# Two buffers lent to the attention's transposed probabilities, and six units under way in place of four, from unit 16 to unit 33

## The chip, the core and the metric

The kernel runs on one core of a Trainium2 chip. Its engines each work through a list of their own, in order: TensorE (PE, matrix products), VectorE (DVE), ScalarE (ACT), GpSimd (POOL) and SyncE (SP, which here issues nearly all transfers of the DMA). An instruction that waits holds up everything behind it on its engine. The metric is the device time of one execution in microseconds (us), lower being better.

## What is computed

Attention over hash buckets, then two dense layers of 1536 tokens:

```python
mask = q_bucket[:, :, :, None] == k_bucket[:, :, None, :]   # 6 sign bits of q @ proj, k @ proj
scores = np.where(mask, scale * np.matmul(q, k.transpose(0, 1, 3, 2)), -1e9)
attn = softmax(scores)                     # B, H, S, D = 2, 8, 768, 64
x = np.matmul(attn, v)                     # -> 1536 x 512
h = x @ w_in;  x = np.where(h > 0, h, np.exp(np.minimum(h, 0)) - 1) @ w_out     # 512 -> 2048 -> 512
h = x @ w_in2; out = (s * np.maximum(h, 0)**2 + b) @ w_out2
```

## The kernel before

Most numbers are split into a high and a low half in 16-bit floating point, and a product is then three products of halves.

**Units.** The attention is cut into 96 units: one unit is one head's 128 queries against all 768 keys. Eight units (all heads) make a chunk of 128 tokens, so there are 12 chunks. Units 0 to 15 (chunks 0 and 1) transpose their probabilities on PE. From unit 16 (`U0`) on, a unit goes through these steps:

1. `u_s`, line 384: four matmuls make the scores `s` in one of two PSUM buffers (`NS = 2`).
2. `u_soft`: DVE caps them and copies them to `p` with their extreme `mx` (line 395), POOL scales `mx` (line 396), ACT takes the exponential in place (line 397). There are three `p` buffers.
3. `u_split`: ACT writes the high half `ph` (line 416), POOL the low half (line 419), and SP issues a transposing DMA into `pt` (line 421). There are three `ph` buffers and four `pt` buffers (`PT = 4`).
4. `u_av`: 18 matmuls of `pt` with the values give the unit's share of `xacc` (line 440).

After the eighth unit of a chunk, `u_norm` divides by the sums: DVE writes `xf` (line 462) and, in chunks 0 and 1, casts the high half `xh` (line 474), POOL subtracts the low half (line 475), and SP issues two transposes (line 479; line 482 in later chunks) into the layer input `xx`. `xx` has three blocks of 512 tokens, each 128 partitions by 8192 bytes; block 0 holds chunks 0 to 3, block 1 chunks 4 to 7.

**The order.** `attention()` (line 518) is a generator. In a round it splits the last unit, runs `u_av` of the oldest unit if `nxt["lag"]` units are under way, and starts the next unit if fewer than that are. The lag is 5 for the first units, 4 from unit 16 on, and 5 again when the weights of the first layer are all in (`w1_step`, line 894, which then also lends further buffers). The first layer (`moe1`, line 613) works on blocks of 256 tokens: `up(0)` makes `h` (16 groups of 12 matmuls, line 574, two groups to a PSUM bank; two banks until the weights are in), ACT and DVE turn `h` into `g` (lines 582, 584, 591), `down(0)` makes `x2p`. `moe1` hands out credit by its matmuls: one unit for each 1.2 us of it during `up(0)`, then one for each 2.5 us. `up(0)` starts in the program when unit 15 has been through `u_av` and `u_norm`.

**Weights.** In the same stretch `w_stream` (line 184) takes in 64 weight chunks of 512 KB as 64-bit numbers: SP loads `wraw` (line 175, three buffers), DVE joins the words in three instructions (lines 213, 214, 216: `wx`, `wx`, `wa`), ACT takes the high half, and DVE (line 223: `wil`, `wol`) or POOL the low half. One step of it follows each step of the attention before `up(0)`, and later two of three slots of `moe1`.

The program is put in order at build time by a scheduler with priorities (program order) and a timing model of its own, so what stands on each engine is not quite the order of the code.

Of the kernel before, what the change touches and what calls it, by code (L numbers as in the profile page):

```python
# [7 lines left out]
F32 = mybir.dt.float32  # L8
# [10 lines left out]
PT = 4  # L19
EX = dict(p=1, ph=1, pt=1, raw=2)  # L20
NP = 3
# [17 lines left out]
NPH = 3  # L39
# [24 lines left out]
W_FROM = 3  # L64
HOLD = {(0, 2, "v"): 3, (0, 3, "v"): 4, (1, 0, "k"): 8, (1, 0, "q"): 9}
HOLD_E = []
LN2 = 0.6931471805599453


def model_kernel(tc, q, k, v, proj, w_in, w_out, w_in2, w_out2, s2, b2, sel, pop, eye, out):  # L70
    nc = tc.nc
    B, H, S, D = q.shape
# [22 lines left out]
    with ExitStack() as base:  # L95
# [13 lines left out]
        unp = right(ast, "unp", NP)  # L109
        un3 = right(ast, "un3", NPH)  # L110
        ptp = right(ast, "ptp", PT)
# [7 lines left out]
        class Ring:  # L119
            def __init__(self):  # L120
                self.sets, self.n = {}, {}
# [5 lines left out]
            def take(self, kind, shape, dt, name):  # L127
                pools = self.sets[kind]
                self.n[kind] += 1
                tag = "m" if kind == "w" else kind  # L130
                return pools[self.n[kind] % len(pools)].tile(shape, dt, tag=tag, name=name)

        class late_by:
            def __init__(self, n):
# [8 lines left out]
        ring = Ring()  # L143
# [22 lines left out]
        def behind(n):  # L166

            return tc.issue_after(w_loads[n]) if n is not None else nullcontext()
# [9 lines left out]
        def w_early(ch, x):  # L178
            t = xx[1].rearrange("p a t -> p (a t)").bitcast(I32)[:, 1024 * x:1024 * x + 1024]
            with behind(HOLD_E[x]):  # L180
                nc.sync.dma_start(out=t.rearrange("p (k n) -> p k n", k=ch[1].shape[1]), in_=ch[1])
# [193 lines left out]
        sps, pf, pt, sums, xacc = ({} for _ in range(5))  # L375
# [12 lines left out]
        def u_soft(u):  # L388
            b, c, h, hp, j = unit(u)
            gr, sl = group(u)  # L390
            if sl == 0:
                sums[gr] = sml.tile([128, H], F32, tag="sum", name="sum")
            f = ring.take("p", [128, S], F32, "p")
            mx = sml.tile([128, 1], F32, tag="mx", name="mx")
            nc.vector.tensor_scalar(f, sps.pop(u), CLAMP, None, op0=ALU.min, op1=ALU.min, accum_out=mx)  # L395
            (nc.gpsimd if U0 <= u < MXP else nc.vector).tensor_scalar(mx, mx, sm / (SQ * SQ), 10.0 * LN2, op0=ALU.mult, op1=ALU.add)  # L396
            nc.scalar.activation(out=f, in_=f, func=ACTF.Exp, scale=-sm / (SQ * SQ), bias=mx,  # L397
                                 accum_out=sums[gr][:, sl:sl + 1])
            pf[u] = f

        def u_split(u, eng):
            f = pf.pop(u)
            if u < FC * H:
                p = ps_p[0].tile([128, S], F32, tag="s", name="pT")
                for cc in range(C):
                    nc.tensor.transpose(p[:, 128 * cc:128 * cc + 128], f[:, 128 * cc:128 * cc + 128], ident)  # L406
                o = ring.take("pt", [128, S], F32, "pt")
                if eng == "act":
                    nc.scalar.activation(out=o, in_=p, func=ACTF.Copy)
                else:  # L410
                    nc.vector.tensor_copy(out=o, in_=p)
                pt[u] = o
                return
            t = ring.take("ph", [128, 2, S], F16, "ph")
            if eng == "act":
                nc.scalar.activation(out=t[:, 0, :], in_=f, func=ACTF.Copy)  # L416
            else:
                nc.vector.tensor_copy(out=t[:, 0, :], in_=f)
            nc.gpsimd.tensor_tensor(out=t[:, 1, :], in0=f, in1=t[:, 0, :], op=ALU.subtract)  # L419
            o = ring.take("pt", [128, 2 * C, 128], F16, "pt")  # L420
            nc.sync.dma_start_transpose(out=o, in_=t.rearrange("p x s -> p (x s)"))
            pt[u] = o

        def u_av(u):
            b, c, h, hp, j = unit(u)
            gr, sl = group(u)
            if sl == 0:
                xacc[gr] = ps_x.tile([128, H, D], F32, tag="x", name="xacc")
            acc = xacc[gr][:, sl, :]
            o = pt.pop(u)  # L430
            if u < FC * H:
                vv = raws[b, hp, "v"].rearrange("p h (c d) -> p h c d", d=D)
                for cc in range(C):
                    nc.tensor.matmul(acc, o[:, 128 * cc:128 * cc + 128], vv[:, j, cc, :],  # L434
                                     start=(cc == 0), stop=(cc == C - 1))
                return
            vv = vHL[b, hp]
            for z, (x, y) in enumerate(((0, 0), (0, 1), (1, 0))):
                for cc in range(C):
                    nc.tensor.matmul(acc, o[:, C * x + cc, :], vv[:, j, cc, y, :],  # L440
                                     start=(z == 0 and cc == 0), stop=(z == 2 and cc == C - 1))

        xx = [xs_.tile([128, 2 * KM, 512], F16, name=f"x{i}") for i in range(B * C // 4)]
# [11 lines left out]
        def u_norm(ch):  # L455
            sm_, acc = sums.pop(ch), xacc.pop(ch)
            rs = sml.tile([128, H], F32, tag="rs", name="rs")
            nc.vector.tensor_scalar(rs, sm_, 1e-9 * SPR, (1.0 if ch < FC else SV) / SX, op0=ALU.add, op1=ALU.mult)
            rr = sml.tile([128, H, 1], F32, tag="rr", name="rr")
            nc.vector.reciprocal(out=rr, in_=rs.rearrange("p (h o) -> p h o", o=1))  # L460
            xf = ring.take("p", [128, H, D], F32, "xf")
            nc.vector.tensor_tensor(out=xf, in0=acc, in1=rr.to_broadcast([128, H, D]), op=ALU.mult)
            if ch < FC:
                xh = per.tile([128, FC, 2, H * D // FC], F16, tag="xh", name="xh")
                fl = xf.rearrange("p (c h) d -> p c (h d)", c=FC)
                hi, lo = xh[:, :, 0, :], xh[:, :, 1, :]
            else:
                xh = per.tile([128, 2, 2, H * D // 2], F16, tag="xh", name="xh")
                fl = xf.rearrange("p (y h) d -> p y (h d)", y=2)
                hi, lo = xh[:, :, 0, :], xh[:, :, 1, :]  # L470
            if FC <= ch < C:
                nc.scalar.activation(out=hi, in_=fl, func=ACTF.Copy)
            else:
                nc.vector.tensor_copy(out=hi, in_=fl)
            nc.gpsimd.tensor_tensor(out=lo, in0=fl, in1=hi, op=ALU.subtract)
            if ch < FC:
                k2 = KM // FC
                for c in range(FC):
                    nc.sync.dma_start_transpose(out=xx[0][:, 2 * k2 * ch:2 * k2 * ch + 2 * k2, 128 * c:128 * c + 128],
                                                in_=xh[:, c].rearrange("p z n -> p (z n)"))  # L480
                return
            nc.sync.dma_start_transpose(out=xx[ch // 4][:, :, ch % 4 * 128:ch % 4 * 128 + 128], in_=xh.rearrange("p y z d -> p (y z d)"))
# [29 lines left out]
        nxt = {"s": 0, "av": 0, "soft": [], "split": [], "lag": LAG0}  # L512
# [5 lines left out]
        def attention():  # L518
            for i in range(-PRE, 0):
                for fn, a in sched.get(i, []):  # L520
                    fn(*a)
                yield
            while nxt["av"] < NU:
                if nxt["split"]:
                    u_split(nxt["split"].pop(0), SPLIT(nxt["s"]))
                u = nxt["av"]
                if u < nxt["s"] and u in pt and (nxt["s"] - u >= nxt["lag"] or nxt["s"] == NU):
                    u_av(u)
                    nxt["av"] += 1
                    if u % H == H - 1:  # L530
                        u_norm(u // H)
                        if u >= FC * H - 1:
                            done_chunks[0] = u // H + 1
                u = nxt["s"]
                if u < NU and u - nxt["av"] < nxt["lag"]:
                    if u == U0:
                        ring.use(p=[unp], ph=[un3], pt=[ptp])
                        nxt["lag"] = PT
                    u_s(u)
                    nxt["s"] += 1  # L540
                    yield
                    u_soft(u)
                    nxt["split"].append(u)
                    for fn, a in sched.get(u, []):
                        fn(*a)
                yield
# [305 lines left out]
        if True:  # L852
# [12 lines left out]
            n, early = 0, []  # L865
            co1 = w_col_chunks(lambda: wo, w_out)
            for _ in att:
                n += 1
                if len(early) < len(HOLD_E) and len(w_loads) > HOLD_E[len(early)]:
                    early.append(w_early(co1[len(early)], len(early)))  # L870
# [155 lines left out]
```

## Time and profile before

| | |
|---|---|
| median of three runs | 709.73 us (708.51 to 713.6) |
| the profiled execution | 714.04 us, of which the profile's span is 711.8 |
| PE busy | 659.6 us, 93% of the span |
| DVE busy | 520.5 us, 73% |
| ACT busy | 416.3 us, 58% |
| POOL busy | 266.1 us, 37% |
| DMA queue of SP | 88.63 MB, 57.4% of 16 engines' span |

The shares are means over stages with different limits. Up to about 75 us the kernel loads and prepares; units 16 to 33 lie at about 90 to 160 us; the rest of the attention runs beside the first layer up to about 395 us; the second layer follows. A row of waits names the engine that waited, the line, and the work whose end released it. The DMA share counts the time of packets, which can overlap on one engine, so it can exceed 1.

### The profile page before, as it was taken

How to read it: one execution, taken by the hardware profiler on the slowest of the kernel's cores; microseconds unless marked ns; L12 is line 12 of the kernel's file. 1: busy time of each engine (PE TensorE's matmuls, PEld its weight loads, DVE VectorE, ACT ScalarE, POOL GpSimd, SP SyncE). 2: the span in 40 equal slices, each digit the busy share in tenths (PEclk: the TensorE clock that was granted, in tenths of full speed). 3: DMA queues.
4: the chain of work that ended last, by engine and by line, in shares of the span. 5: the costliest groups of instructions: out<-in, count | busy, mean ns of one | idle time of the engine just before them, and what ended most of it. 6: DMA issues, size and time to landing. Idle time of an engine off the chain costs nothing.

```text
span 711.8 us, 15212 instructions
## 1 busy us (share of the span) xinstructions
PE 659.6 (93%) x6192; PEld 506.6 (71%) x6192; DVE 520.5 (73%) x893; ACT 416.3 (58%) x687; POOL 266.1 (37%) x211
## 2 busy tenths in 40 slices
PE   2598978879989999999999999999999999999998
PEld 0286857668767777888888988874444446888887
DVE  5779989998878568645644699339999626999730
ACT  2849768966778788656755333234545525555520
POOL 0136767776345469945855421311211200000000
PEclk9769999999999999999999999999999999999999
DMA  9965699999999669977668555014443000000100
GB/s 211 299 162 170 160 203 203 223 228 225 196 211 216 116 116 171 150 125 122 119 115 117 135 162 165 1 31 119 135 138 112 0 1 1 16 31 31 45 30 30
DMA packets 206805, 89.72 MB, mean 126 GB/s; under 512 B 171920, under 2 KB 203408, under 8 KB 206736
## 3 DMA queue, kind: packets, MB, share of 16 engines
q1 hardware_dynamic: 206144, 88.63, 57.4%
q8 instruction: 48, 0.79, 0.5%
q14 instruction: 21, 0.17, 0.1%
q10 hardware_dynamic: 592, 0.14, 0.1%
HBM read 43.13 MB, written 3.15 MB: 65 GB/s over the span
## 4 chain that ended last, share of the span: by engine, by line
PE 66%; DMA 10%; DVE 10%; ACT 7%; issue 5%; SPq 1%; POOL 1%; DVEq 0%; ACTq 0%; POOLq 0%
PE h L574 27%; PE y L818 15%; PE x2p L574 12%; DMA pt<-ph 6%; PE s L384 4%; PE xacc L440 3%; PE xacc L434 2%; DVE p L395 2%; ACT p L397 1%; PE pT L406 1%; ACT ph L416 1%; DMA q<-src 1%; DVE g L591 1%; DMA raw<-in_k 1%; ACT q L357 1%
## 5 line engine op out<-in xcount | busy, mean ns | idle before, releaser
L419 POOL TENSOR_TENSOR ph<-p,ph 128x768 f16<-128x768 f32 x80 | 134.6, 1686 | 79.2 <-ACT ph L416 44.3
L574 PE MATMUL h<-x,wih 128*128 128x256 f16 x768 | 131.3, 275 | 3.0 <-DVE g L591 1.5
L574 PE MATMUL h<-x,wi 128*128 128x512 f16 x576 | 124.5, 379 | 0.0
L395 DVE TENSOR_SCALAR_CACHE_REDUCE p<-s 128x768 f32<-128x768 f32 x96 | 91.0, 951 | 42.2 <-PE s L384 41.3
L397 ACT ACTIVATE p<-p,mx 128x768 f32<-128x768 f32 x96 | 89.2, 929 | 50.6 <-DVE mx L396 38.8
L818 PE MATMUL y<-wqh,a 128*128 128x256 f16 x672 | 110.3, 273 | 0.0
L818 PEld LDWEIGHTS <-a 128*128 128x128 f16 x1008 | 98.6, 98 | 11.7
L574 PE MATMUL h<-x,wil 128*128 128x256 f16 x384 | 105.4, 275 | 0.0
L574 PE MATMUL x2p<-gh,woh 128*128 128x256 f16 x384 | 104.1, 273 | 0.8 <-ACT gh L594 0.8
L574 PE MATMUL x2p<-gl,woh 128*128 128x256 f16 x384 | 104.5, 273 | 0.1
L574 PEld LDWEIGHTS <-wi 128*128 128x128 f16 x576 | 56.4, 98 | 67.7
L574 PE MATMUL x2p<-gh,wol 128*128 128x256 f16 x384 | 104.5, 273 | 0.0
L818 PE MATMUL y<-wql,a 128*128 128x256 f16 x336 | 91.1, 273 | 0.0
L384 PE MATMUL s<-k,q 128*128 128x512 f16 (+1 forms) x384 | 80.7, 335 | 8.0 <-DVE p L395 7.9
L574 PEld LDWEIGHTS <-wih 128*128 128x128 f16 x768 | 74.9, 99 | 15.2 <-issue 2.0
L574 PEld LDWEIGHTS <-woh 128*128 128x128 f16 x768 | 74.9, 98 | 11.6
L597 POOL TENSOR_TENSOR gl<-g,gh 128x512 f16<-128x512 f32 x48 | 59.0, 1229 | 61.0 <-ACT gh L594 60.7
L440 PE MATMUL xacc<-vv,pt 128*128 128x64 f16 x1440 | 57.6, 194 | 16.1 <-DMA pt<-ph 16.1
L416 ACT ACTIVATE ph<-p 128x768 f16<-128x768 f32 x80 | 66.7, 836 | 7.7 <-DMA pt<-ph 5.2
L440 PEld LDWEIGHTS <-pt 128*128 128x128 f16 x1440 | 53.5, 99 | 24.3 <-DMA pt<-ph 20.3
L610 DVE SCALAR_TENSOR_TENSOR g<-h,sbs,r 128x512 f32<-128x512 f32 x48 | 35.7, 745 | 23.6 <-ACT r L607 23.6
L384 PEld LDWEIGHTS <-q 128*128 128x128 f16 x384 | 34.5, 100 | 25.6 <-issue 10.8
(118 smaller groups left out, 1040.8 us busy)
## 6 DMA issues: line engine op xcount, KB each, us to landing
wraw<-in_moe_w_in SPq DMA_DIRECT2D x32, 512.0 KB, 3.9
wraw<-in_moe_w_out SPq DMA_DIRECT2D x32, 512.0 KB, 3.9
out<-y SPq DMA_DIRECT2D x10, 256.0 KB, 2.0
raw<-in_k SPq DMA_DIRECT2D x6, 384.0 KB, 4.8
raw<-in_q SPq DMA_DIRECT2D x6, 384.0 KB, 5.7
v<-in_v SPq DMA_DIRECT2D x4, 384.0 KB, 7.8
pt<-ph SPq DMA_TRANSPOSE x80, 4.1
x<-in_k SPq DMA_DIRECT2D x2, 384.0 KB, 5.0
```

The costliest lines, as they stand in the source:

```text
L357: nc.scalar.activation(out=o[r, j].rearrange("p c t -> p (c t)"), in_=p[r], func=ACTF.Relu, scale=sc, bias=pop_sb[r, x:x + 1])
L384: nc.tensor.matmul(p[:, a0:a1], w[b, hp][:, j, c, :], kf[:, a0:a1], start=(x == 0), stop=(x == 1))
L395: nc.vector.tensor_scalar(f, sps.pop(u), CLAMP, None, op0=ALU.min, op1=ALU.min, accum_out=mx)
L397: nc.scalar.activation(out=f, in_=f, func=ACTF.Exp, scale=-sm / (SQ * SQ), bias=mx, accum_out=sums[gr][:, sl:sl + 1])
L416: nc.scalar.activation(out=t[:, 0, :], in_=f, func=ACTF.Copy)
L419: nc.gpsimd.tensor_tensor(out=t[:, 1, :], in0=f, in1=t[:, 0, :], op=ALU.subtract)
L434: nc.tensor.matmul(acc, o[:, 128 * cc:128 * cc + 128], vv[:, j, cc, :], start=(cc == 0), stop=(cc == C - 1))
L440: nc.tensor.matmul(acc, o[:, C * x + cc, :], vv[:, j, cc, y, :], start=(z == 0 and cc == 0), stop=(z == 2 and cc == C - 1))
L574: nc.tensor.matmul(p, ws[a](kk), xs[b](kk), start=(kk == 0 and z == 0), stop=(kk == n_kk - 1 and z == 2))
L597: nc.gpsimd.tensor_tensor(out=gl, in0=t["g"], in1=gh, op=ALU.subtract)
L610: nc.vector.scalar_tensor_tensor(out=g, in0=p, scalar=sb["s"], in1=t["r"], op0=ALU.mult, op1=ALU.mult)
L818: nc.tensor.matmul(p, a[:, xa, kk, :], wq[y][:, WQ[n], kk, :], start=first and k == 0, stop=k == 3 * K2 - 1, skip_group_check=True)
```

## The change

From unit 16 on the ring of `pt` buffers gets two more: slices of 3072 bytes per partition of `xx[1]`, the second block of the layer input, into which nothing else is written before chunk 4 (units 32 to 39) is done. At the same place the lag becomes 6 in place of 4. When unit 34 starts, the ring and the lag are set back to what they were. The numbers of `p` and `ph` buffers stay (`p=0, ph=0`). Units 19, 20, 25, 26, 31 and 32 get the lent buffers.

```diff
+X1 = dict(p=0, ph=0, pt=2)
+X1_END = 34
...
+        class Guest:
+            def __init__(self, t, at, n):
+                self.t, self.at, self.n = t, at, n
+            def tile(self, shape, dt, tag=None, name=None):
...
+                t = self.t[:, self.at // 2:(self.at + n * z) // 2]
...
                     if u == U0:
+                        t, at_, sets = xx[1].rearrange("p a t -> p (a t)"), 0, {}
+                        for k_, p_, n_ in (("p", unp, NP), ("ph", un3, NPH), ("pt", ptp, PT)):
+                            sets[k_] = [p_] * n_
+                            for _ in range(X1[k_]):
+                                sets[k_].append(Guest(t, at_, 4 * S))
+                                at_ += 4 * S
+                        ring.use(**sets)
+                        nxt["lag"] = PT + X1["pt"]
+                    if u == X1_END:
                         ring.use(p=[unp], ph=[un3], pt=[ptp])
                         nxt["lag"] = PT
```

No instruction is added or taken away; the lag and the rings move instructions on every engine. Lines below 67 of the kernel before stand 2 further down in the changed one, from 133 on 19, from 537 on 28.

On SP, from the last load of `w_in` and the first of `w_out` on (`x_113` is block 0 of the layer input and `x_114` block 1, so that `x_114<-ph` is a transpose into a lent buffer), the kernel before has:

```order
L175 DMA wraw<-in_moe_w_out 128x4x256
L421 DMA_TRANSPOSE pt<-ph 128x12x128 x2
L175 DMA wraw<-in_moe_w_out 128x4x256
L479 DMA_TRANSPOSE x_113<-xh 128x4x128 x2
L421 DMA_TRANSPOSE pt<-ph 128x12x128 x3
L175 DMA wraw<-in_moe_w_out 128x4x256 x2
```

The changed one has in the same place:

```order
L194 DMA wraw<-in_moe_w_out 128x4x256
L440 DMA_TRANSPOSE pt<-ph 128x12x128 x2
L194 DMA wraw<-in_moe_w_out 128x4x256 x2
L440 DMA_TRANSPOSE pt<-ph 128x12x128
L440 DMA_TRANSPOSE x_114<-ph 128x12x128
L498 DMA_TRANSPOSE x_113<-xh 128x4x128 x2
L440 DMA_TRANSPOSE x_114<-ph 128x12x128
L194 DMA wraw<-in_moe_w_out 128x4x256 x2
```

The two transposes of chunk 1 into the layer input (`x_113<-xh`) now stand behind those of units 18 and 19 and behind one more weight load.

On DVE, from the scores of unit 18 (the first `p,mx<-s` here) to those of unit 21, the kernel before has:

```order
L395 TENSOR_SCALAR p,mx<-s 128x768
L462 TENSOR_TENSOR xf<-xacc,rr 128x512
L216 SCALAR_TENSOR_TENSOR wa<-wraw,wx 128x512
L474 CAST xh<-xf 128x2x256
L395 TENSOR_SCALAR p,mx<-s 128x768
L213 TENSOR_SCALAR wx<-wraw 128x512
L223 SCALAR_TENSOR_TENSOR wil<-wa,wih 128x512
L395 TENSOR_SCALAR p,mx<-s 128x768
L214 SCALAR_TENSOR_TENSOR wx<-wraw,wx 128x512
L395 TENSOR_SCALAR p,mx<-s 128x768
```

The changed one has, from unit 19 (the first `p,mx<-s` here) to unit 21, behind unit 18 and the two instructions `wa` and `wx`:

```order
L414 TENSOR_SCALAR p,mx<-s 128x768
L233 SCALAR_TENSOR_TENSOR wx<-wraw,wx 128x512
L242 SCALAR_TENSOR_TENSOR wil<-wa,wih 128x512
L235 SCALAR_TENSOR_TENSOR wa<-wraw,wx 128x512
L414 TENSOR_SCALAR p,mx<-s 128x768
L232 TENSOR_SCALAR wx<-wraw 128x512
L481 TENSOR_TENSOR xf<-xacc,rr 128x512
L242 SCALAR_TENSOR_TENSOR wil<-wa,wih 128x512
L233 SCALAR_TENSOR_TENSOR wx<-wraw,wx 128x512
L493 CAST xh<-xf 128x2x256
L414 TENSOR_SCALAR p,mx<-s 128x768
```

The normalisation of chunk 1 (`xf`, then the cast `xh`) now stands behind the scores of units 19 and 20 and six weight instructions.

On PE the kernel before has the scores up to unit 21, then line 440 of unit 16, 12 matmuls of `h`, line 440 of unit 17, the scores of unit 22 and 36 matmuls of `h`. The changed one has the scores up to unit 23, then line 440 of units 16, 17 and 18, 12 matmuls of `h`, line 440 of unit 19, the scores of unit 24 and the same 36 matmuls of `h`.

## Rows read from the trace of the kernel before

**Rows 1.** Stretches: length, busy PE, PEld, DVE, ACT, POOL, granted clock, DMA share, GB/s.

```profile
90.00:105.00 15.00, 10.23 (x95) 7.47 (x95) 13.65 (x26) 9.91 (x18) 11.54 (x12) 0.89 1.00 194
105.00:120.00 15.00, 13.56 (x179) 11.07 (x178) 12.87 (x22) 12.81 (x24) 9.34 (x9) 1.00 1.04 216
120.00:150.00 30.00, 26.19 (x323) 21.58 (x323) 29.83 (x52) 25.46 (x46) 25.41 (x24) 1.00 1.05 214
150.00:165.00 15.00, 11.96 (x141) 9.38 (x139) 13.15 (x24) 10.94 (x21) 9.16 (x11) 0.89 1.14 240
165.00:300.00 135.00, 125.53 (x1519) 102.54 (x1518) 100.13 (x191) 107.40 (x182) 82.74 (x59) 1.00 0.95 174
300.00:450.00 150.00, 150.00 (x1707) 131.36 (x1706) 96.82 (x186) 78.15 (x134) 71.81 (x51) 1.00 0.63 128
```

**Rows 2.** Waits of PE, 105 to 165 us: us in total, times, longest.

```profile
PE xacc L440 <- DMA pt<-ph: 7.0, 6, 2.4
PE h L574 <- DVE g L591: 1.0, 1, 1.0
```

**Rows 3.** Chain of work that ended last, 90 to 165 us: start, us, what.

```profile
99.02 4.11 DMA x<-xh
103.17 2.15 PE h L574 x18
...
124.64 5.62 DMA pt<-ph
130.31 0.70 PE xacc L440 x18
...
138.47 5.38 DMA pt<-ph
143.93 0.84 ACT ph L416
```

**Rows 4.** Timeline of DVE: start, us, work, [idle before it <- releaser].

```profile
94.14 0.69 DVE L462 TENSOR_TENSOR xf<-xacc,rr 128x512 f32<-128x512 f32 x1
94.74 0.68 DVE L216 SCALAR_TENSOR_TENSOR wa<-wraw,wx 128x512 int32<-128x512 int32 x1
95.33 0.42 DVE L474 CAST xh<-xf 128x512 f16<-128x512 f32 x1
95.67 0.95 DVE L395 TENSOR_SCALAR_CACHE_REDUCE p<-s 128x768 f32<-128x768 f32 x1
...
108.14 0.69 DVE L591 SCALAR_TENSOR_TENSOR g<-h,e 128x512 f32<-128x512 f32 x1 [2.09 <-ACT e L584]
```

**Rows 5.** Timeline of PE around the start of `up(0)`.

```profile
94.28 0.81 PE L384 MATMUL s<-k,q 128*128 128x512 f16 x4 [1.28 <-DVE p L395]
97.09 1.14 PE L440 MATMUL xacc<-vv,pt 128*128 128x64 f16 x18 [2.01 <-DMA pt<-ph]
98.05 0.61 PE L574 MATMUL h<-x,wih 128*128 128x256 f16 x2
100.36 0.69 PE L440 MATMUL xacc<-vv,pt 128*128 128x64 f16 x18
103.17 0.39 PE L574 MATMUL h<-x,wih 128*128 128x256 f16 x2 [1.48 <-DMA x<-xh]
```

**Rows 6.** Timeline of POOL there.

```profile
95.84 1.16 POOL L475 TENSOR_TENSOR xh<-xf,xh 128x512 f16<-128x512 f32 x1 [1.09 <-DVE xh L474]
```

**Rows 7.** DMA issues, 105 to 165 us, then 300 to 380: count, size, landing us.

```profile
pt<-ph SPq DMA_TRANSPOSE x16, 4.9
...
pt<-ph SPq DMA_TRANSPOSE x22, 3.8
```

**Rows 8.** Waits, 90 to 165 us, of SP's queue and of ACT.

```profile
SPq L421 <- POOL mx L396: 17.8, 9, 3.0
...
ACT ph L416 <- DMA pt<-ph: 2.0, 2, 1.1
```

More of the change, by code (lines that the diff above doesn't have):

```diff
@@ L131, in take @@
                 return pools[self.n[kind] % len(pools)].tile(shape, dt, tag=tag, name=name)
+        class Guest:
+            def __init__(self, t, at, n):
+                self.t, self.at, self.n = t, at, n
+            def tile(self, shape, dt, tag=None, name=None):
+                z = 4 if dt == F32 else 2
+                n = 1
+                for d in shape[1:]:
+                    n *= d
+                assert n * z <= self.n
+                t = self.t[:, self.at // 2:(self.at + n * z) // 2]
+                t = t.bitcast(F32) if z == 4 else t
+                if len(shape) == 3:
+                    t = t.rearrange("p (a b) -> p a b", a=shape[1])
+                return t
         class late_by:
```

## The prediction

> **What bounds the kernel now.** I read the stretches first. From 300 us on PE is busy in every microsecond [rows 1], so whatever units 16 to 33 gain or lose reaches the end of the kernel at full size: the first layer stands behind them on PE, and no engine gives it back. The profiled execution took 714.04 us, with a span of 711.8; it lies 4.3 above the median of 709.73, so I work out a difference there and carry it to the median.
>
> Between 90 and 165 us PE is idle for 4.77, 1.44, 3.81 and 3.04 us, 13.1 in all [rows 1]. Second, the waits of PE: from 105 to 165 us, 7.0 us in six waits are line 440 waiting for a transpose `pt<-ph` to land, and 1.0 is `h` waiting for `g` [rows 2]. This is what more buffers and a longer lag are aimed at: a unit's `u_av` asked of PE two units later gives its transpose two more units' time to land.
>
> Two things speak against taking the 7.0 us whole. DVE is busy 12.87, 29.83 and 13.15 us in the 60 from 105 to 165 [rows 1]: 4.15 us idle, and 0.17 in the middle 30. A unit needs its 0.95 us of DVE for its scores [rows 4], the weight chunks need theirs, and no lag shortens either. And in the chain of waits the long transposes end in two ways: at 130.31 on PE, in line 440, but at 143.93 on ACT, in line 416, which writes `ph` [rows 3]. There the unit waits for one of the three `ph` buffers to be read out, and the change lends none of those. ACT's own waits of this kind come to 2.0 us [rows 8].
>
> **The change, part by part.** It adds no instruction. The two slices of `xx[1]` are free until chunk 4 is done, and the readers of a lent buffer (line 440 of units up to 32) stand on PE long before that, so I cost the lending itself at nothing; what covers it is the distance from unit 32 to unit 39, seven units. If that were gone, one transpose of the layer input would wait for one unit's 18 matmuls, 0.69 us [rows 5].
>
> *The start, unit 16 to 24.* Here the order costs something. In the kernel before, DVE does `xf` of chunk 1 at 94.14 us and the cast `xh` at 95.33, POOL follows at 95.84, SP issues the two transposes, the second at 99.02, it lands 4.11 us later, and the 36 matmuls of `h` that need it start at 103.17 after a wait of 1.48 [rows 3 to 6]. In the changed order the scores of units 19 and 20 and six weight instructions stand ahead of `xf` on DVE, and two more weight instructions in place of one between `xf` and the cast. A weight instruction starts 0.6 us after the one before (94.14, 94.74, 95.33), a unit's scores take 0.95 [rows 4]: 6 x 0.6 + 2 x 0.95 + 0.6 = 6.1 us. DVE was never short of work there (13.65 of 15 busy [rows 1]), so no idle time swallows this. On POOL the low halves of units 18 and 19 now come before that of `xh`, and on SP their transposes and a weight load come before its two; these are done while DVE is still busy with those 6.1 us, so I add nothing for them. The 36 matmuls then start at 103.17 + 6.1 = 109.3.
>
> PE is not idle for all of that. Ahead of the 36 matmuls it now also does the scores of units 23 and 24 and line 440 of units 18 and 19: 2 x 0.81 + 2 x 0.69 = 3.0 us [rows 5], which it need not do later. The start costs 6.1 - 3.0 = 3.1 us. Bounds: nothing, if DVE alone sets the pace up to 150 us and PE catches up in its gaps; and 6.1, if the work done ahead is worth nothing, because units were fitted into gaps anyway.
>
> The scores of units 22 and 23 need one of two PSUM buffers, so they wait for DVE's scores of units 20 and 21, and line 440 of unit 16, at 97.09 before, now stands behind both: PE has a longer gap ahead of it. After its gap of 2.01 us the kernel before ran its first 12 matmuls of `h` from 98.05 to 100.36, 2.31 us [rows 5], where 18 of them later took 2.15 [rows 3], so 12 would take 1.43. The 0.9 us between are the lower of its two clock levels, 1.2 in place of 2.4 GHz, as the granted clock of 0.89 over that stretch says [rows 1]. The same matmuls run in both kernels after a gap, so I add nothing, and 0.9 to the upper bound.
>
> *Units 20 to 33.* Of the 7.0 us of waits [rows 2] I take what DVE has to spare, 4.15 us, since the nearest row to a limit is DVE's 29.83 of 30; half of it is one wait, 2.09 us at 108.14 for the first group of `up(0)` [rows 4], and in the changed order scores and weight instructions stand ahead of that `g` to fill it. The lower bound is nothing: if the `ph` buffers hold the units back, their transposes are late all the same. The upper bound is 7.0. On PE the changed order in fact puts line 440 only about one unit later than before in the middle of the stretch, and around unit 33 at the old place, because the lag falls back to 4 at unit 34.
>
> *Behind unit 34.* Lag and rings are the old ones, and the units run at most one ahead of before against the first layer. PE's idle time from 165 to 300 is 9.5 us [rows 1]; I leave it as it is.
>
> **Sum.** 3.1 - 4.15 = -1.05 us: 713.0 for the profiled execution, **708.7 us** for the median.
>
> **The rivals.** *Faster.* The waits are latency and nothing else, and the start is hidden behind DVE: 0 for the start, and all 7.0 of the waits go: 702.7. For it speaks that the wait for `pt` is by far PE's largest; against it DVE's 4.15 us and the `ph` row. The Trainium skill, "Perfetto Trace Analysis", section "Optimization Strategy", says that the same gap repeating on the engine that should be saturated can mean that there isn't buffer enough for the next tile. By that rule the six waits would go and this rival would be right; the trace agrees that the gap repeats, and does not yet show which buffer is the short one. Chance 0.22.
>
> *No gain, only the start.* The transposes are slow because the DMA is full, and two more in flight only land later. The DMA share is 1.04 to 1.14 from 105 to 165 us [rows 1], and a transpose lands in 4.9 us there against 3.8 in the quiet stretch [rows 7]. Or the `ph` buffers hold the pace. Then the change doesn't do what it says: 709.73 + 3.1 = 712.8. Against it: SP waited for POOL before issuing, 17.8 us in nine waits on one row alone [rows 8], so the queue is not always backed up. The skill's same page, section "What 'DMA-bound' means", says that where specific DMA engines or the issuing queue bind, large descriptors are what matter; by it lent buffers are worth nothing here. The trace speaks only half for it, by that wait of SP. Chance 0.22.
>
> *Slower.* The start is paid in full: `up(0)` starts 6.1 us late, the two units done ahead only fill gaps that were there, and PE runs 0.9 us more at the lower clock: 709.73 + 7.0 = 716.7. The place is the wait for `x<-xh` ahead of the 36 matmuls; it decides from the point where this wait ends later than about 107 us, 4 us later than now. For it speaks the row of 4.11 us for the landing, which nothing shortens; against it DVE's full rows behind it, in which PE has 3.81 us to catch up [rows 1]. Chance 0.16.
>
> **How the numbers follow.** The forecast has 0.40: its parts are each half certain, and it lies between the others. The range reaches to the faster and the slower rival, since signs are mixed: 703.0 to 716.7; the forecast's own is 706 to 711.5. About 1%, 7.1 us, is what a measurement of this kernel can tell from no change: under 702.6 lies near half of the faster rival, 0.11; over 716.8 some more than half of the slower one and a little of the second, 0.11; the rest, 0.78, is within.
>
> **What would show it.** The start: the cast `xh` near 101.4 us, the second `x<-xh` landing near 109, and line 440 of unit 16 behind the scores of unit 23. If the cast is at 97 or before, the 3.1 us are wrong. The middle: PE's waits for `pt<-ph` from 105 to 165 us down to about 3 us, and DVE with almost no idle time; if they stay near 7 with ACT waiting more in line 416, the `ph` buffers hold; if the landing goes from 4.9 towards 6 us, the DMA does. I am wrong in kind if PE's idle time behind 165 us moves by more than 2 us, since I gave that stretch nothing.

## The result, and the profile after

The changed kernel takes 719.16 us (median of four runs, 717.42 to 722.22), the kernel before 711.55 beside it (708.51 to 713.6): a ratio of 1.011, with a 95% interval of 1.0067 to 1.0154. It is slower by 1.1%, 7.6 us, where I had forecast 708.7 and a range up to 716.7. The profiled execution took 722.22 us, its span 720.4.

The stretches of the changed kernel, as in [rows 1] (length, busy PE, PEld, DVE, ACT, POOL, granted clock, DMA share, GB/s):

```profile
90.00:105.00 15.00, 7.95 (x78) 5.42 (x77) 14.97 (x28) 8.98 (x16) 9.99 (x12) 0.67 1.00 219
105.00:120.00 15.00, 12.89 (x146) 10.03 (x145) 11.99 (x22) 11.76 (x22) 8.17 (x8) 0.88 1.03 189
120.00:150.00 30.00, 26.10 (x325) 21.38 (x323) 28.46 (x49) 26.22 (x49) 24.60 (x24) 1.00 1.13 235
150.00:165.00 15.00, 14.21 (x174) 11.85 (x172) 14.72 (x23) 10.58 (x19) 11.91 (x11) 1.00 1.14 226
165.00:235.00 70.00, 59.44 (x661) 46.84 (x659) 50.09 (x91) 53.19 (x89) 29.69 (x25) 0.95 1.00 187
235.00:300.00 65.00, 62.35 (x784) 51.67 (x783) 41.47 (x93) 50.28 (x87) 47.20 (x32) 1.00 0.84 143
300.00:450.00 150.00, 149.17 (x1711) 129.98 (x1710) 92.84 (x187) 79.06 (x134) 72.04 (x51) 1.00 0.63 130
```

And two stretches of the kernel before, cut in the same way:

```profile
165.00:235.00 70.00, 63.94 (x742) 51.92 (x741) 57.50 (x97) 52.89 (x89) 33.95 (x26) 1.00 1.05 205
235.00:300.00 65.00, 61.59 (x779) 50.62 (x778) 42.63 (x95) 54.51 (x94) 48.79 (x33) 1.00 0.84 140
```

From 90 to 165 us PE idles 7.05 + 2.11 + 3.90 + 0.79 = 13.85 us, where it was 13.1 [rows 1]. From 165 to 235 us PE idles 10.56 us in place of 6.06 and does 661 matmuls in place of 742, part of them at the lower of its two clock levels (granted clock 0.95). That row of before is a favourable one: e3_ph2, which has its order on PE, and e9_norm_early (both below) show no loss and idle 9.34 and 9.15 us there, at a granted clock of 1.00:

```profile
165.00:235.00 70.00, 60.66 (x712) 48.74 (x709) 56.62 (x94) 53.81 (x90) 30.72 (x25) 1.00 1.00 193
165.00:235.00 70.00, 60.85 (x720) 48.73 (x719) 53.24 (x91) 53.77 (x90) 30.41 (x24) 1.00 0.97 198
```

So of that stretch the clock and 1 to 2 us of idle time belong to the change. A comparison from a point of the program is surer than one by the time since the span began. DVE's order is the same in all kernels here up to the scores of unit 18; from their start to the end of the span, before first:

```profile
93.26:711.80 618.54, 592.04 (x5724) 456.48 (x5723) 447.38 (x738) 354.55 (x588) 228.61 (x172) 0.99 0.55 115
91.16:720.40 629.24, 596.70 (x5724) 458.96 (x5723) 441.65 (x738) 355.04 (x588) 227.65 (x172) 0.98 0.54 113
```

PE does the same 5724 matmuls in 10.7 us more: 6.0 us more idle time (32.54 against 26.50), and 4.7 us more for the matmuls themselves, at a lower mean granted clock. The stretch repeats well: before, e3_ph2 and e4_pt2_lag4, which have one order on PE, take 618.54, 618.78 and 618.08 us for it, while their whole spans differ by 3.5 us. Its first part, up to the scores of unit 36, before first:

```profile
93.26:156.86 63.60, 53.17 (x641) 43.24 (x641) 60.03 (x103) 49.92 (x89) 48.41 (x46) 0.97 1.07 218
91.16:156.96 65.80, 53.02 (x626) 42.45 (x625) 61.00 (x104) 50.12 (x90) 49.14 (x47) 0.90 1.08 219
```

It is 2.2 us longer, and 34 matmuls of the first layer fewer are done in it (table below), some 4 us at the 2.15 us for 18 of [rows 3]. By this estimate half of the 10.7 us or more arises here, and the rest behind unit 36.

The waits of PE in the changed kernel, first from 105 to 165 us, which answers to [rows 2], then from 165 to 235:

```profile
PE xacc L459 <- DMA pt<-ph: 6.6, 5, 2.7
...
PE s L403 <- DVE p L414: 3.4, 2, 2.4
PE xacc L459 <- DMA pt<-ph: 3.4, 2, 3.2
PE pone L372 <- DVE bits L362: 2.9, 2, 1.7
PE pone L372 <- DVE p L414: 0.7, 1, 0.7
```

The six waits of 7.0 us are now five of 6.6. Lines 362 and 372 prepare the hash buckets of the second batch; in the kernel before they cost PE 0.6 us in the second of the two stretches (but 2.4 us in e9_norm_early, which has no loss):

```profile
PE xacc L440 <- DMA pt<-ph: 3.7, 3, 1.7
PE s L384 <- DVE p L395: 0.7, 1, 0.7
PE pbit L340 <- DMA q<-src: 0.6, 1, 0.6
PE pone L353 <- DVE bits L343: 0.6, 2, 0.4
PE h L574 <- DVE g L591: 0.5, 1, 0.5
```

The start on DVE, which answers to [rows 4] (first the scores of unit 18 in the kernel before; then, in the changed one, scores of units 18, 19, 20, then `xf`, the cast, and the first `g`):

```profile
93.26 0.95 DVE L395 TENSOR_SCALAR_CACHE_REDUCE p<-s 128x768 f32<-128x768 f32 x1
...
91.16 0.95 DVE L414 TENSOR_SCALAR_CACHE_REDUCE p<-s 128x768 f32<-128x768 f32 x1
...
93.36 0.95 DVE L414 TENSOR_SCALAR_CACHE_REDUCE p<-s 128x768 f32<-128x768 f32 x1
...
96.03 0.95 DVE L414 TENSOR_SCALAR_CACHE_REDUCE p<-s 128x768 f32<-128x768 f32 x1
...
97.50 0.68 DVE L481 TENSOR_TENSOR xf<-xacc,rr 128x512 f32<-128x512 f32 x1
...
99.69 0.41 DVE L493 CAST xh<-xf 128x512 f16<-128x512 f32 x1
...
115.64 0.68 DVE L619 SCALAR_TENSOR_TENSOR g<-h,e 128x512 f32<-128x512 f32 x1
```

And on PE, which answers to [rows 5]:

```profile
94.36 0.87 PE L403 MATMUL s<-k,q 128*128 128x512 f16 x4 [1.38 <-DVE p L414]
97.04 1.44 PE L403 MATMUL s<-k,q 128*128 128x512 f16 x4 [1.80 <-DVE p L414]
98.27 2.12 PE L459 MATMUL xacc<-vv,pt 128*128 128x64 f16 x36
102.98 1.14 PE L459 MATMUL xacc<-vv,pt 128*128 128x64 f16 x18 [2.58 <-DMA pt<-ph]
103.93 0.61 PE L602 MATMUL h<-x,wih 128*128 128x256 f16 x2
106.47 1.16 PE L459 MATMUL xacc<-vv,x 128*128 128x64 f16 x18
107.45 1.39 PE L403 MATMUL s<-k,q 128*128 128x512 f16 x4
108.68 0.38 PE L602 MATMUL h<-x,wih 128*128 128x256 f16 x2
```

This profiled execution is 2.1 us earlier than that of before by unit 18 (91.16 against 93.26), so I count from there: the cast comes 8.5 us later, where it was 2.1; the first `h` 12.8 in place of 4.8; the first `g` 24.5 in place of 14.9. Three gaps of PE (1.38, 1.80 and 2.58 us) stand ahead of the first `h`, and from the second of them to the 36 matmuls at 108.68 PE runs at the lower level: 1.44 and 1.39 us for scores that take 0.81 [rows 5], 1.16 for 18 matmuls that take 0.69.

### The profile page after: what moved, and what is told of

It reads as the page before. It is cut to its first block, busy times and chain, and to the rows that moved or that the text cites. A ratio compares the mean times of both kernels' runs of the same rounds, so it can differ in the third digit from the quotient of the medians.

```text
span 720.4 us, 15215 instructions
## 1 busy us (share of the span) xinstructions
PE 660.5 (92%) x6192; PEld 505.8 (70%) x6192; DVE 515.4 (72%) x893; ACT 417.0 (58%) x687; POOL 265.1 (37%) x211
## 4 chain that ended last, share of the span: by engine, by line
PE 53%; DVE 6%; DMA 2%; ACT 2%; issue 1%; POOL 0%; DVEq 0%; ACTq 0%; POOLq 0%; SPq 0%
PE h L602 23%; PE y L846 15%; PE x2p L602 8%; PE s L403 3%; PE xacc L459 3%; DMA pt<-ph 1%; DVE e L617 1%; DVE g L619 1%; DVE wx L232 1%; DVE wx L233 1%; DVE wa L235 1%; ACT gh L622 1%; DMA wraw<-in_moe_w_in 1%; DVE wi L242 1%; DMA x<-xh 0%
## 5 line engine op out<-in xcount | busy, mean ns | idle before, releaser
L403 PE MATMUL s<-k,q 128*128 128x512 f16 (+1 forms) x384 | 82.7, 341 | 16.9 <-DVE p L414 16.1
L602 PEld LDWEIGHTS <-wih 128*128 128x128 f16 x768 | 75.1, 99 | 11.6 <-issue 0.3
L459 PE MATMUL xacc<-vv,pt 128*128 128x64 f16 x1332 | 53.2, 195 | 14.7 <-DMA pt<-ph 14.5
L459 PEld LDWEIGHTS <-pt 128*128 128x128 f16 x1332 | 49.8, 99 | 21.6 <-DMA pt<-ph 18.3
L403 PEld LDWEIGHTS <-q 128*128 128x128 f16 x384 | 35.0, 101 | 36.4 <-issue 22.2
```

The costliest lines, as they stand in the source:

```text
L403: nc.tensor.matmul(p[:, a0:a1], w[b, hp][:, j, c, :], kf[:, a0:a1], start=(x == 0), stop=(x == 1))
L602: nc.tensor.matmul(p, ws[a](kk), xs[b](kk), start=(kk == 0 and z == 0), stop=(kk == n_kk - 1 and z == 2))
```

## The experiments

My theory after this was that the late start explains the loss, and its rival that the longer lag itself does harm, or that another buffer is the short one. The table lists all runs by ratio to the kernel before. "Start" is whether chunk 1 is normalised where it was or about two units later. The last columns say how many matmuls of the first layer (`h` + `x2p`) stand on PE ahead of the scores of unit 36 and of unit 94, counted in the built programs.

| kernel | start | lag, 22 to 33 | unit 36 | unit 94 | ratio, 95% interval |
|---|---|---|---|---|---|
| before | early | 4 | 254 | 1512 | 1 |
| changed | late | 6 | 220 | 1488 | 1.011 (1.0067 to 1.0154) |
| e1_late_start | early | 6 | 234 | 1536 | 0.9977 (0.9948 to 1.0007) |
| e9_norm_early | early | 6 | 234 | 1536 | 0.9972 (0.9946 to 0.9998) |
| e16_lag6_to_38 | early | 6 | 234 | 1536 | 1.0016 (0.9992 to 1.0041) |
| e3_ph2 | early | 4 | 254 | 1512 | 1.0015 (0.9985 to 1.0044) |
| e4_pt2_lag4 | early | 4 | 254 | 1512 | 1.0009 (0.9979 to 1.004) |
| e7_pt1_lag5 | late | 5 | 192 | 1500 | 1.0111 (1.006 to 1.0162) |
| e10_start_only | late | 4 | 217 | 1488 | 1.0185 (1.0147 to 1.0223) |
| e11_norm_late | late | 4 | 192 | 1464 | 1.0195 (1.0151 to 1.0239) |
| e14_layer_late | layer alone late | 4 | 212 | 1464 | 1.0161 (1.013 to 1.0192) |
| e19_ahead | early | 4 | 254 | 1536 | 1.0025 (1.0 to 1.005) |
| e19_behind_1 | early | 4 | 235 | 1488 | 1.0103 (1.0058 to 1.0147) |
| e19_layer_behind | early | 4 | 228 | 1464 | 1.0136 (1.0108 to 1.0165) |
| e18_catch_up_1 | late | 6 | 226 | 1512 | 1.0067 (1.0041 to 1.0092) |
| e18_catch_up_2 | late | 6 | 226 | 1536 | 1.0104 (1.0065 to 1.0142) |
| e18_catch_up | late | 6 | 229 | 1632 | 1.0113 (1.0085 to 1.014) |

### Is it the start, the lag, or a buffer?

**e1_late_start.** Lag and rings change only when chunk 1 is through:

```diff
                     if u == U0:
+                        ring.use(p=[unp], ph=[un3], pt=[ptp])
+                        nxt["lag"] = PT
+                    if u > U0 and nxt["av"] >= U0 and not nxt.get("lent"):
+                        nxt["lent"] = True
```

> The change, but the two buffers and the lag of 6 begin only when unit 16 is about to go through u_av, that is once chunk 1 has been normalised; until then the lag is 4 and the rings are those of before. On DVE xf and the cast of chunk 1 stand where they stood before (behind the scores of unit 18), on PE line 440 of unit 16 stands behind the scores of unit 21. Theory A, the loss is made at the start (chunk 1's normalisation behind units 19 and 20, PE idle and at its lower clock there): the loss of 7.6 us goes, 709 to 713 us, and the 36 matmuls of h start within 1 us of before, counted from the scores of unit 18. Theory B, the loss is made behind unit 34 by the other order: it stays, 716 to 719. If the lag of 6 itself is worth what the prediction took for it (4.15 us) and A holds: 707 to 709.

Measured: 711.1 us beside 712.69 for before, 0.9977. The loss is gone with the late start. Taken alone, this also looks as if lag 6 were worth nothing: the interval includes 1. With e9 below, which has the same order on every engine, it is a small gain.

**e7_pt1_lag5.** Half the change:

```diff
-X1 = dict(p=0, ph=0, pt=2)
+X1 = dict(p=0, ph=0, pt=1)
```

> Half the change: one lent buffer and a lag of 5 from unit 16 on. On PE line 440 of units 16 and 17 stand behind the scores of unit 22, one unit fewer on each count than in the change. Theory A: about half of the loss, 714 to 717 us, the first layer starting 3 to 4 us late. Theory B: anything, since the order behind unit 34 is a third one.

Measured: 719.97, 1.0111. A miss: half the change costs as much as the whole. The cast was 6.0 us behind unit 18's scores and the first `g` 19.9, about half of the delay; so the delay at the start isn't by itself the measure of the loss (the shorter lag behind it may also give back less; that was not taken apart).

**e3_ph2 and e4_pt2_lag4.** The kernel before, its order on PE unchanged, with two lent buffers for `ph` (`X1 = dict(p=0, ph=2, pt=0)`) or for `pt` (`pt=2`), at lag 4 (`nxt["lag"] = PT`).

> The lag stays 4 and the order on PE and DVE is that of before; the two slices of the second block are lent to the high and low halves ph (five buffers in place of three) and not to pt. Theory C, the three ph buffers hold the units back (ACT line 416 waiting for a transpose, 2.0 us from 90 to 165): these waits go and 1 to 2 us with them, 709 to 711 us. If ph is not the short buffer: 711 to 712, no difference.

> The two buffers are lent to pt as in the change, but the lag stays 4, so the order on every engine is that of before. All theories: no difference from before, 711 to 712 us; the lag and not the buffer decides when a transpose is issued and read. A loss here of over 2 us would say that the place of the lent buffers costs something.

Measured: 713.09 and 712.72, both the time of before. Lending costs nothing that these runs can tell, and at lag 4 neither ring is the short one.

**e11_norm_late.** The kernel before, with nothing of the change but its effect on chunk 1:

```diff
+                if "held" in nxt and nxt["s"] >= U0 + 5:
+                    u_norm(nxt.pop("held"))
+                    done_chunks[0] = FC
...
+                        if u == FC * H - 1:
+                            nxt["held"] = u // H
+                        else:
+                            u_norm(u // H)
...
```

> The kernel before, lag 4, no lent buffer; only chunk 1's normalisation (xf, xh and what follows, up to x<-xh) is asked for two units later, as the change did it. Theory A (the whole loss comes from this late normalisation: the layer input is late, and line 440 of unit 16 waits for xf, since there is one xacc buffer): the cast xh comes 8 to 9 us behind unit 18's scores on DVE in place of 2.1, and the time is 717 to 721. Theory B (the start costs only what PE loses in its first 15 us there, 2.3 us of idle time and about 2.3 of lower clock; the rest comes from the longer lag behind it): 714 to 717.

**e10_start_only.** The changed kernel with `X1_END = 22`.

> The changed kernel, but lag 6 and the lent buffers end at unit 22 in place of 34: only the start differs from the kernel before. Theory A: the loss is that of the changed kernel, 717 to 721. Theory B: 714 to 717, since units 22 to 33 run at lag 4 as before.

**e9_norm_early.** The changed kernel, one condition more:

```diff
-... (nxt["s"] - u >= nxt["lag"] or nxt["s"] == NU):
+... (nxt["s"] - u >= (PT if u < U0 else nxt["lag"]) or nxt["s"] == NU):
```

> The changed kernel, lag 6 and two lent buffers for units 16 to 33, but line 440 of units up to 15, and so chunk 1's normalisation, goes at lag 4 as before. Theory A: the cast xh is back at 2 us behind unit 18's scores, and the time is that of the kernel before or up to 1 us below it, 710 to 713. Theory B (lag 6 over units 22 to 33 costs 3 us or more by itself): 714 to 717. If the gain that I had forecast for the longer lag is there once the start is mended: 707 to 709.

Measured: 725.13, 724.22 and 709.59 us, beside 711.63 for before. The late normalisation alone, without a longer lag, costs 13.5 us, more than either theory gave it; without it the change gains 2.0 us, and its interval ends just below 1. e1 and e9 differ only in which units get the lent buffers, so they measure one order twice, 0.9977 and 0.9972: an estimate from both is a gain of 0.1 to 0.4%. So the start is the harm, and lag 6 in units 22 to 33 is worth something. With the late start it is worth more: from e10 to the changed kernel 0.0075, 5.3 us, though their intervals just touch, and from e11 0.0085, 6.0 us, though e11 also has the layer 24 matmuls further behind at unit 94.

**e16_lag6_to_38.** e9 with `X1_END = 38`.

> The changed kernel with chunk 1 closed at lag 4 (the version with the early normalisation), and lag 6 and the lent buffers up to unit 38 in place of 34. If the longer lag is worth something by itself where the start is mended, four more units of it give up to 1 us more: 708.5 to 709.5. If it is worth nothing by itself: 709 to 712, as before.

Measured: 713.11, 1.0016, above both ranges. Four more units of lag 6 take the gain away again. Why is open.

### What in the late start costs?

**e14_layer_late.** `xf` of chunk 1 stays where it was, so `xacc`, of which there is one buffer, is free for unit 16; what follows `xf` is asked for two units later (`u_norm` cut in two, the second part held as in e11).

> The kernel before, lag 4, no lent buffer; xf of chunk 1 stays where it was, so the one xacc buffer is free for unit 16 on time; only what follows it (xh, x<-xh, and the first matmuls of h) is asked for two units later. On DVE the cast keeps its place all the same; on PE the scores of units 22 and 23 and line 440 of unit 17 now stand ahead of the first h. Theory C (the loss of the late normalisation comes through xacc: line 440 of unit 16 waits for xf, and PE stands idle and then runs at the lower clock): 710 to 714, and the granted clock from unit 18's scores on is that of the kernel before. Theory D (it comes from the first layer's start standing two units later, whatever xacc does): 717 to 725.

Measured: 724.7, 1.0161. The cast kept its place on DVE (2.1 us behind unit 18), the first `g` came 16.9 us behind it, 2 later than before, and the fifth where it was (36.5 against 36.4). PE's idle time from 90 to 165 us is 12.5, less than before. All the same, nearly the whole loss is there. What this kernel shares with e11 is that the layer's program begins two units later. The stretches of e14 behind the start:

```profile
165.00:235.00 70.00, 59.76 (x633) 46.20 (x629) 51.39 (x90) 51.94 (x87) 28.27 (x23) 0.93 1.00 192
235.00:300.00 65.00, 62.09 (x790) 50.78 (x788) 41.64 (x90) 49.36 (x86) 45.92 (x32) 1.00 0.80 135
300.00:450.00 150.00, 145.78 (x1663) 126.62 (x1661) 95.02 (x183) 76.40 (x131) 70.88 (x50) 1.00 0.64 128
```

Much of it shows there: a clock of 0.93 and 10.2 us of idle time from 165 to 235 (8 to 9 us, at a clock of 1.00, in kernels without a loss such as e3, e4 and e9), and 4.2 us idle from 300 to 450, where before had none [rows 1].

**e19.** That is the place of the layer in the order, so I moved it alone (and with it the weight chunks, which go by the layer's slots), in the kernel before, by the credit with which `moe1` begins to pay for steps of the attention:

```diff
-            credit = 0.0
+            credit = 2.6
```

> The kernel before with its start, lag and buffers untouched (the cast xh 2 us behind unit 18's scores); only the credit starts at +2.6 in place of 0, so the attention runs two units further ahead of the first layer: 192 and 36 matmuls of h and x2p at unit 36 in place of 192 and 62, 384 and 376 at unit 54 in place of 387 and 384, 696 of x2p at unit 94 in place of 744. Theory E (the place): 717 to 725. Theory F (the late start): 710 to 713.

Measured: 720.84, 1.0136. The start is that of before (the cast 2.1 us behind unit 18, the first `g` 14.8), and the layer up to two units further behind costs 9.3 us beside 711.56 for before.

**e19_behind_1 and e19_ahead.** Half the step (1.3), and a step to the other side (-1.3):

> The kernel before, start, lag and buffers untouched; the credit starts at +1.3 in place of 0, half of the step that gave 1.0136: 192 and 43 matmuls of h and x2p at unit 36 in place of 192 and 62, 720 of x2p at unit 94 in place of 744, which is where the changed kernel has it. If the cost goes with the place step by step: 714 to 718. If it came from one spot that the larger step happened to hit: 711 to 713.

> The kernel before with the credit at -1.3: up to unit 38 the same order, then the first layer one unit further ahead, 768 of x2p at unit 94 in place of 744, as in the version with the early normalisation and lag 6 (e9). If the 0.3 % that e9 gained came from the place and not from the longer lag: 708.5 to 710.5. If from the lag: 711 to 714.

Measured: 718.78 (1.0103) and 713.28 (1.0025). Behind costs, and half the step costs most of what the whole one does (its 718.78 is just above my range for step by step); ahead gains nothing. So the 0.3% of e9 doesn't come from the place. e19_behind_1 and e9 have nearly the same place of the layer from line 440 of unit 28 to that of unit 62 (by that of unit 30: 192 of `h` with 37 and 42 of `x2p`; by unit 42, 302 and 192 in both), at lag 4 and lag 6. Behind it they part: by unit 94 e9 has the layer 48 matmuls further ahead. Their stretches from 120 to 165 us, and PE's waits in them, e19_behind_1 first:

```profile
120.00:165.00 45.00, 36.89 (x422) 29.33 (x421) 39.21 (x66) 32.94 (x60) 31.30 (x31) 0.90 1.04 198
```

```profile
PE xacc L440 <- DMA pt<-ph: 8.1, 5, 3.6
```

And e9:

```profile
120.00:165.00 45.00, 39.92 (x490) 32.58 (x488) 43.60 (x73) 35.99 (x65) 33.44 (x33) 1.00 1.06 218
```

```profile
PE xacc L459 <- DMA x<-ph: 2.0, 2, 1.3
PE xacc L459 <- DMA pt<-ph: 1.9, 4, 0.6
```

Here the longer lag does what it was thought to do: 8.1 us of waits for transposes become 3.9 (those into lent buffers are called `x<-ph`), and PE stays at its upper clock. The times differ by 1.0103 - 0.9972 = 0.0131, 9.3 us, but part of that is the place behind unit 62. Nor is 8.1 what the kernel before waits. In the same stretch it and e1, which has the order of e9, have:

```profile
PE xacc L440 <- DMA pt<-ph: 5.7, 5, 2.4
PE xacc L459 <- DMA pt<-ph: 4.7, 7, 1.4
```

Against the kernel before, the longer lag takes 1.0 and 1.8 us off these waits, which goes with the 1.6 and 2.0 us that e1 and e9 gain.

**e18.** The changed kernel with its late start, the credit at -7.8, -1.3 and -2.6, so that the layer catches up.

> The changed kernel with everything in its start as it is (the late normalisation, lag 6, lent buffers); only the credit, the count by which the first layer pays for steps of the attention, starts at -7.8 in place of 0, so the first layer catches up: by the scores of unit 54 PE has done 387 matmuls of h and 384 of x2p, as in the kernel before, where the changed kernel has done 384 and 331. Theory E (the loss comes from the first layer standing two units further behind in the order on PE, all the way): 710 to 714. Theory F (it is the late start itself, its idle time and lower clock): 718 to 721.

> The same with the credit at -1.3: up to unit 62 the order is nearly that of the changed kernel (384 and 330 at unit 54), from unit 70 on the first layer stands where it stood in the kernel before (744 matmuls of x2p at unit 94, where the changed kernel has 720). If the place counts at units 36 to 60: 718 to 721. If the place at the end counts: 711 to 714.

> The changed kernel, its late start as it is, with the credit at -2.6: at units 38 and 40 the first layer is where the kernel before has it (192 and 93, 192 and 120), at unit 58 too (387 and 384), at unit 94 24 matmuls further (768). If the place is the whole loss: 710 to 713. If the start keeps its part (PE's idle time from 90 to 120 us and the lower clock there, some 3 to 5 us): 714 to 717. If catching up costs the units as much as it gives: 718 to 721.

Measured: 720.33 (1.0113), 715.73 (1.0067) and 719.12 (1.0104). The smallest step seems to give back 0.4%, though its interval overlaps that of the changed kernel; larger ones cost the units what they give the layer: with -7.8 unit 95's scores come 308.6 us behind unit 18's, where the changed kernel has them at 299.2 and the one before at 293.6. None of them brings the time of before back. By what I had expected, -7.8 came out for the late start itself, as e19 had for the place; -1.3 fell between its two ranges, and -2.6 into the range in which catching up costs what it gives.

## Why the prediction was wrong

**What bounds it.** That a loss reaches the end held for the changed kernel: PE's idle time from 300 to 450 us went from 0 to 0.83, and PE's idle time and its slower matmuls are the whole of the 10.7 us behind unit 18. But PE isn't full there whatever the order: it idles 4.2 us in e14 and 3.6 in e11.

**The start.** Its first step held. I had 6.1 us for what stands ahead of the cast; it came 6.4 later (8.5 - 2.1), and DVE worked without a gap, as I said (14.97 of 15). The lower clock I had put into the upper bound as 0.9, since "the same matmuls run in both kernels after a gap". They are not the same: scores and `u_av` of more units now stand between the gaps. Over [rows 5] that is 0.63 + 0.58 for two units' scores, 0.74 for line 459 of units 16 and 17 (2.12 against 2 x 0.69), 0.47 for unit 19's: 2.4 us.

**The step that failed** is the sum of that part, 6.1 - 3.0 = 3.1, with an upper bound of 7. The part measures 13.5 us by e11 and 12.6 by e10, whose layer is at unit 94 just as far behind as that of the changed kernel. I had taken the start for a delay that is paid once, where it stands, and the two units done ahead as work saved. But the credit hands out units in a fixed ratio to the layer's matmuls, and the layer is let in by unit 15's end. When that comes two units later, the units stay ahead for the rest of the attention: at unit 94, 24 matmuls of the layer fewer stand ahead in the changed kernel, 48 fewer in e11. This changes the order on PE for as long as both run, and it alone, at lag 4 and with the start untouched, costs 7.2 us (e19_behind_1) and 9.3 (e19_layer_behind). The work done ahead was no credit but the debt. And the delay itself cost PE more than 3.1 us: by the estimate under the rows up to unit 36, half of the 10.7 us or more stands there.

**Units 20 to 33.** The sign was right; the size, 4.15 us, is not shown. With the start as it was, which is what I had priced, the longer lag gains 1.6 us (e1) and 2.0 (e9), and e9's interval ends at 3.8; with the late start it is worth 5.3 and 6.0 by e10 and e11 against the changed kernel. That 4.15 lies between is luck. The row by which I wanted to see it goes with the smaller size: the waits went from 7.0 to 6.6 in the changed kernel, and from 105 to 165 us they are 6.1 in e1 and 5.3 in e9, not about 3. I limited the gain by DVE's idle time; that limit was not shown, since DVE did less, not more, from 120 to 150 us (28.46 against 29.83).

**Behind unit 34.** I gave this stretch nothing, because "the units run at most one ahead of before against the first layer". In the built programs it is more: 34 matmuls of the layer fewer stand ahead of unit 36, 56 fewer ahead of unit 54 (384 and 331 of `h` and `x2p` in place of 387 and 384), where a step of one unit, e19_behind_1, is 24 at unit 94. I had named idle time moving by more than 2 us there as what would make me wrong in kind, and from 165 to 300 us it went from 9.5 to 13.2. That sign is worth less than I thought: e3, with before's order on PE, idles 11.6 us there, e9, which gains, 12.0, and e16, at the time of before, 13.2.

**The rivals.** "Slower" came nearest with 716.7, by the right place and the wrong mechanism: its wait for `x<-xh` is no longer there at all ahead of the 36 matmuls at 108.68. PE was at work until then, and the landing that "nothing shortens" took 2.5 us in place of 4.11. Of "no gain, only the start" the reasons show little; `ph` buffers were lent at lag 4 alone (e3). The landing of transposes from 105 to 165 us in the changed kernel, as in [rows 7], and ACT's waits for `ph` from 90 to 165, as in [rows 8]:

```profile
pt<-ph SPq DMA_TRANSPOSE x12, 5.4
x<-ph SPq DMA_TRANSPOSE x5, 4.9
```

```profile
ACT ph L435 <- DMA pt<-ph: 0.9, 2, 0.5
ACT ph L435 <- DMA x<-ph: 0.6, 1, 0.6
```

5.4 and 4.9 us against 4.9 is half a microsecond at most, and ACT's waits fell from 2.0 us to 1.5. "Faster" had beside it a rule of the Trainium skill, "Perfetto Trace Analysis", section "Optimization Strategy", that a repeated gap can mean too few buffers. The runs agree in part: buffers without more units under way do nothing (e4, 1.0009), and with them, start kept, the waits shrink (7.0 to 5.3 from 105 to 165 us in e9) and don't go.

**What stays open.** No single wait carries the price of the layer's place: e14 pays from 165 to 235 and from 300 to 450 us, e19_behind_1 from 120 to 165 (PE busy 36.89 of 45 at a clock of 0.90). Nor is it settled how much of the changed kernel's loss is place and how much late start. e11 and e14 differ by the late cast and `xacc`, 0.0034, but their intervals overlap. The traces point to both, one execution each. Between the scores of unit 18 and unit 36 the seven kernels with a late cast (the changed one, e7, e10, e11 and the three e18) idle 11.8 to 14.3 us on PE, at a granted clock of 0.85 to 0.92; the seven with the cast in time and the layer not behind by credit (before, e1, e3, e4, e9, e16, e19_ahead) idle 8.1 to 10.9 at 0.94 to 1.00; e14 and the two e19 behind lie between, 10.8 to 12.5 at 0.92 to 0.97. So catching up leaves the start's own price standing, as e18 measured.

## What to carry to other kernels

Where two streams of work are interleaved by a count, and one of them is let in by a point of progress of the other, a longer lag moves that point, and with it every instruction behind it: price it by the order over the whole overlap, not by the delay at the start alone. Set the longer lag behind that point (e9: one condition, 0.9972 in place of 1.011) and the loss is gone and a small gain kept. Compare two traces from the last instruction that stands at the same place in both programs, not from the start of the span: the three executions of one order differed by 0.7 us so, and by 3.5 in their spans. And before a tuned order is moved, move it a step to each side by itself: that costs two runs and says how steep the place is.

## What the runs showed of the hardware

PE's clock is not a property of the order alone. From 90 to 105 us the granted clock was 0.89 in the kernel before [rows 1], 0.67 in the changed one and 1.00 in e19_layer_behind; in e1 and e9, which have the same order on every engine, it was 0.77 and 0.89 (0.94 and 0.97 from the scores of unit 18 to those of unit 36):

```profile
90.00:105.00 15.00, 13.40 (x156) 10.58 (x157) 12.36 (x24) 12.27 (x23) 9.83 (x11) 0.77 1.10 229
```

```profile
90.00:105.00 15.00, 11.39 (x118) 8.63 (x118) 12.94 (x24) 11.05 (x20) 10.60 (x11) 0.89 1.07 209
```

What ran at the lower of the two levels in the changed kernel's start took 1.5 to 1.8 times its usual time (2.12 us for 36 matmuls that take 1.38, 1.44 for scores that take 0.81). And the lower level came back far from the start, with 0.95 from 165 to 235 us, where I had looked for idle time alone.
